# Batches 2 and 3 of a block-sparse attention: gathered keys and value rows, groups of 64 queries

## The chip, the core and the metric

The kernel runs on one core of one Trainium2 chip. A core has five engines that work side by side and wait for each other by semaphores: TensorE (PE, matmuls; its weight loads are shown as PEld), VectorE (DVE), ScalarE (ACT), GpSimd (POOL) and SyncE (SP, which here only issues DMAs). The metric is the device time of one execution in microseconds, as a median over runs.

## What is computed

Attention with a block mask (4 batches, 8 heads, 768 positions, 64 numbers per head), and then a layer of two matrix products on its output. Blocks are 32 positions long, so there are 24. A query block sees its own block and the two beside it, the first and the last block, and three blocks that a table names for it; the first and the last query block see everything.

```
scores = scale * q @ k.T
mask = abs(blk_i - blk_j) <= 1
mask = mask | (blk_i == 0) | (blk_j == 0) | (blk_i == 23) | (blk_j == 23)
for qb in range(24):
    for kb in sampled_blocks[qb]:              # 24 x 3 table
        mask[block qb, block kb] = True
attn = softmax(where(mask, scores, -1e9))
x = (attn @ v), heads side by side             # 3072 x 512
h = x @ w_in                                   # 512 x 2048
out = (max(h, 0) ** 2) @ w_out                 # 2048 x 512
```

## The kernel before

The numbers q, k and v are loaded by pairs of heads (a "unit" u; 16 units, four to a batch), cast to bf16 (`cast_qk`, `cast_v`) and transposed, so that QK holds queries and keys with the 2 x 64 numbers of the pair on the 128 partitions. Units 0 to 3 are transposed by TensorE, the others by DMA (`transp_dma`). In the loads, 6 successive positions lie on one partition, so a chunk of 128 keys holds every sixth position, from all blocks. No chunk can therefore be left out for a query, and the mask is laid over the full scores.

For each unit and each third of the queries (256) `scores` multiplies them with all six chunks of 128 keys; the two heads of a pair use the upper and the lower 64 rows of the PE array, by the helper `pair` (all its matmuls stand at L173). `exps` (L318) takes the exponential of two chunks at a time, 1024 numbers per partition, into pT. `masks` (L325) multiplies pT by the 0/1 mask MK, which is made once from the table by small matmuls; in the first third of batch 0, the mask is added to the scores instead. `values` multiplies pT by the value rows VT, which have a 65th column of ones, so that the sum of the weights comes along; some of units 0 to 3 use `values_full` (L358), which takes all 128 rows at once, the others the two row halves after each other. `normalize` divides (L365, L367), and the result is transposed into xT, by TensorE in batch 0 and by DMA afterwards.

The second part takes 256 tokens at a time (twelve tiles T). `hidden` multiplies by w_in, `relu` (L430, L432) and `square` (L441, L443) follow on ACT, DVE or POOL, `output` multiplies by w_out, `out_copy` and `store` bring the result out. This work on one batch is interleaved with the attention of the next.

The order of all of this is not left to a scheduler. Each step is a numbered task with its dependencies and buffers; the string PROGRAM lists all of them as words such as `P89/0` or `V24`: engine, task, and place in PSUM. Each engine executes its own words strictly in the order listed, and buffer counts (PT_BUFS, R_BUFS and so on) hold a task back until an older one has left its buffer.

Of the kernel before, what the change touches and what calls it, by code (L numbers as in the profile page):

```python
# [19 lines left out]
P = 128  # L20
# [5 lines left out]
def kernel(  # L26
# [32 lines left out]
    NRAW, NPB, QC_BUFS, XQ_BUFS, YS_BUFS = 4, 6, 5, 4, 3  # L59
    PT_BUFS, R_BUFS, G_BUFS, XT_BUFS, NX = 8, 3, 13, 3, 4  # L60
# [5 lines left out]
    scratch = dram.tile([1, 4], BF, name="scratch")  # L66
    ctx.enter_context(tc.manual_schedule())
# [49 lines left out]

    qv = q.rearrange("b (a t) (p n) d -> b a p t (n d)", t=2, p=P)
# [5 lines left out]
    def load(u, engs, e=None):  # L124
        b, a = divmod(u, HP)
        raw[u] = []
        for name, view, eng in zip(("qs", "ks", "vs"), (qv, kv, vv), engs):
            t = ld.tile([P, 2, NCH, D], F32, name=name, tag=name)
            eng.dma_start(out=t.rearrange("p t n d -> p t (n d)"), in_=view[b, a])
            raw[u].append(t)  # L130
# [5 lines left out]
    def load_part(eng, u, w, ns):  # L136
        if u not in raw:
            raw[u] = [ld.tile([P, 2, NCH, D], F32, name=n, tag=n) for n in ("qs", "ks", "vs")]
        eng.dma_start(out=raw[u][w][:, :, ns].rearrange("p t n d -> p t (n d)"),  # L139
                      in_=(qv, kv, vv)[w][0, u][:, :, ns.start * D:ns.stop * D])  # L140
# [22 lines left out]
    place = consts.tile([P, S], BF, name="place")  # L163
# [28 lines left out]
    QK, VT = [], []  # L192
    for i in range(NPB):
        QK.append(consts.tile([P, 2, S], BF, name=f"QK{i}"))
        VT.append(consts.tile([P, 2, NCH, 72], BF, name=f"VT{i}"))
        G.memset(VT[i][:, :, :, D:VW], 1.0)
# [34 lines left out]
    MK = consts.tile([P, NCH, S], BF, name="MK")  # L231
# [6 lines left out]
    def mask_evac(n, c0, c1, e):  # L238
        pk = mtile.pop((n, c0))
        if e == "ACT":  # L240
            A.activation(out=MK[:, n:n + 2, c0:c1], in_=pk, func=AF.Exp)
        else:
            V.tensor_scalar(out=MK[:, n:n + 2, c0:c1], in0=pk, scalar1=-1.0, scalar2=None, op0=AOP.is_ge)

# [11 lines left out]
    def cast_v(u, e):  # L256
        copy(e, VT[u % NPB][:, :, :, 0:D], raw[u][2])
# [63 lines left out]
    def masks(a, e):  # L321
        u, q0, w, cs = a
        pT = ptile[a].rearrange("p h (c q) -> p h c q", q=w)
        m = MK[:, cs[0]:cs[-1] + 1, q0:q0 + w]
# [5 lines left out]
    def values(slots, crossed, buf, e):  # L330
        u, q0, w, _ = slots[0]
        i = u % NPB
# [5 lines left out]
        for a in slots:  # L338
            pT = ptile.pop(a) if crossed else ptile[a]
            for j, n in enumerate(a[3]):  # L340
                for qc in range(w // P):
                    last = pair(lambda h: po[:, h, qc], lambda h, rows: pT[rows, h, j * w + qc * P:j * w + (qc + 1) * P],
                                lambda h, rows: VT[i][rows, h, n, 0:VW], crossed, start=not crossed and n == 0 and qc == 0,
# [4 lines left out]
    def values_full(slots, buf, e):  # L348
        u, q0, w, _ = slots[0]
        i = u % NPB  # L350
        otile[u, q0] = tile_of(buf)
        po = outs_of(otile[u, q0], w)
        for a in slots:
            pT = ptile.pop(a)
            for j, n in enumerate(a[3]):
                for h in range(2):
                    for qc in range(w // P):
                        nc.tensor.matmul(po[:, h, qc], pT[:, h, j * w + qc * P:j * w + (qc + 1) * P], VT[i][:, h, n, 0:VW],  # L358
# [20 lines left out]

    def x_evac(u, q0, w, e):  # L380
        b, a = divmod(u, HP)
        if b not in xT:
            xT[b] = work.tile([P, HP, S], BF, name="xT", tag="xT", bufs=XT_BUFS)
        copy(e, xT[b][:, a, q0:q0 + w].rearrange("r (c h p) -> r h c p", h=2, p=D), spare_of(otile.pop((u, q0)), w))

    def x_transp_dma(u, q0, w, e):
        b, a = divmod(u, HP)
        if b not in xT:
            xT[b] = work.tile([P, HP, S], BF, name="xT", tag="xT", bufs=XT_BUFS)
        sy.dma_start(out=xT[b][:, a, q0:q0 + w].rearrange("r (c p) -> r c p", p=P),  # L390
                     in_=xtile.pop((u, q0)).rearrange("p c h d -> p (c h d)"), transpose=True)
        otile.pop((u, q0))

# [13 lines left out]
    def hidden(T, f, part, parts, buf, e):  # L407
# [9 lines left out]
        for j, kc in work_[part % (parts // 2) * k_:(part % (parts // 2) + 1) * k_]:  # L417
            hlast[T, f] = pair(lambda i: htile[T, f][:, i, j * w:(j + 1) * w],
                               lambda i, rows: w_in_sb[rows, kc, (f + i * n + j) * P:(f + i * n + j + 1) * P],
                               lambda i, rows: xT[b][rows, kc, c0:c0 + w], crossed,  # L420
# [66 lines left out]
    def store(T, i, y, e):  # L487
        ts, n, cs = y
        sy.dma_start(out=ov[T[0], :, T[1] // P + ts:T[1] // P + ts + n, cs[0]:cs[1]],
                     in_=ystile.pop((T, i)).rearrange("p (n d) -> p n d", n=n))  # L490

# [6 lines left out]
    order = [(b * HP + a, q0, QW, cs) for b in range(B) for q0 in range(0, S, QW) for a in range(HP) for cs in CHUNKS]  # L498
    N0 = len(order) // B
    ev, cv, tr, sc_of, va_of, mu, mk, wl, gate, xb = {}, {}, {}, {}, {}, {}, {}, {}, {}, {}  # L500

    def prepare(u):
# [4 lines left out]
        if u >= HP:  # L507
            g = gate[GATES[min(u - HP, len(GATES) - 1)]]
            ld_t = T_(load, u, (sy, sy, sy), deps=cv[u - NRAW] + tr[u - NRAW] + [g])
# [22 lines left out]

    def attend(a, add):
# [7 lines left out]
        if not add:  # L541
            ex = T_(masks, a, deps=[ex] + [mk[n, c] for n in cs for c in range(q0, q0 + w, P)])
# [17 lines left out]
        kw = {}  # L560
        if b not in xb:
            xb[b] = Buf("xT")
            kw = dict(get=[xb[b]])
# [4 lines left out]
        mu[u, q0] = T_(x_evac, u, q0, w, deps=[xt], put=[ob[u, q0], ot], **kw)  # L568

# [9 lines left out]
    for u in range(NU):  # L579
        sc_of[u], va_of[u] = [], []  # L580
    for us in [range(b * HP, (b + 1) * HP) for b in range(B)]:
# [3 lines left out]
        if us[0] < HP:  # L585
            for c0, c1 in MASKED:
                for n in range(0, NCH, 2):
                    mb = Buf("X")
                    t = T_(mask_tile, n, c0, c1, mb, get=[mb], deps=mr)
                    x = T_(mask_evac, n, c0, c1, deps=[t], put=[mb])  # L590
                    for c in range(c0, c1, P):
                        mk[n, c] = mk[n + 1, c] = x
        for a in mine:
# [3 lines left out]
    for T in TILES:  # L597
        b, c0, tw = T
        n_u = per_unit(T)
        need = [mu[b * HP + a, q0] for a in range(HP) for q0, qw in QT if q0 < c0 + tw and c0 < q0 + qw]  # L600
        for f in range(0, NF, n_u):
            hb, ht, rb, gb = Buf("X"), Buf("H"), Buf("r"), Buf("g")
            last_use = c0 + tw == S and f + n_u == NF
            parts = 4
            hd = []
            for part in range(parts):
# [4 lines left out]
                             put=[xb[b]] if last_use and end else []))  # L611
# [20 lines left out]
        A18 P19/0 V24 P8/1 V21 P0/2 P25/3 P17/1 V20 A1 P6/1 P22/1 V26 G34 A23 P89/0 P9/2 P4/3 P35/1 A90 P12/2 P91/3 V36 V31 P93/2 A92  # L632
        P16/1 V44 P32/0 P13/1 V33 A94 V41 P103/1 P45/3 P42/0 A104 P101/2 V46 V30 P99/3 V54 V43 P95/1 A100 V51 A102 P55/0 P109/3 V56
        V96 P52/0 A110 G61 V53 P113/2 P97 P2/0 V98 A114 G40 P123/3 V3 P119/1 G50 A124 P75/0 P105/2 V76 G62 A120 P111/3 V27 G63 V106
        A112 P28/0 P121/1 G60 V29 P107 P73/0 A122 V108 P5/3 V37 P71/3 P115/2 G57 V74 A72 V47 P81/1 P38/0 P125/3 A82 V39 V116 P135/0
        G67 P11/1 V126 P117 P79/1 A136 V118 G64 V80 P127 P129/2 P132/0 A130 V128 G68 P48/1 V137 P777/3 V49 P778 A133 G65 V131 P142/2
        P58/1 P779 A143 V59 P145/0 V134 P780 P784/1 A146 V144 P161/2 P785 V781 A162 P148/0 P786 P787 A149 V147 G782 P155/2 P138/3 V788
        A156 P791/0 V163 A783 P158/1 P15/2 P792 V150 A159 S69 P174/2 S237 P793 V139 A175 P171/1 V160 P140 P794 V141 A172 V157 P151/2
        V176 A795 P168/3 P164/1 V173 A169 G796 V152 P181/0 V165 A182 P153 P798/3 V154 G66 V170 P166 P799 A797 S70 P184/2 V167 G790
        S243 P201/0 P177/1 A185 G789 A202 P800 V178 S249 P77/2 P801 A78 P179 P212/0 V180 V802 A213 P187/2 P821/1 P822 A188 P827/0 V183  # L640
        G803 P823 V186 A804 P198/3 P828 A199 P209/2 P824 P829 A210 V189 P815/3 V238 P816 A825 P190/2 V211 S239 P830 V214 P191 A831
        P817 V240 P215/1 P818 V192 A216 S241 P805/0 V200 A832 P193 V217 P195/1 P806 V203 A196 P807 V194 A819 V197 P223/2 P808 A224
        G820 P218/1 P204/3 A826 P809 P87/2 P205 G242 V88 P810 V206 G248 P226/2 V246 P219 A227 P207 P811 G250 V208 S247 V220 P229/3
        V244 P833/2 A230 P221 P834 V225 S245 P812 V252 P835 V228 A813 S251 P836 V222 P839/3 V231 A837 S253 P83/1 P264/0 P840 V84 G838
# [74 lines left out]
```

## Time and profile before

| | |
|---|---|
| median of 3 runs | 266.07 us (265.7 to 266.57) |
| profiled execution | 264.27 us, span on the core 262.5 us, granted TensorE clock 0.999 |
| PE busy | 251.1 us (96%), 5452 matmuls |
| ACT busy | 203.5 us (78%), of it 141.3 in 144 exponentials |
| DVE busy | 179.5 us (68%), of it 91.6 in 132 mask multiplications |
| POOL busy | 61.3 us (23%), of it 37.5 in 24 squarings |
| DMA | 37.20 MB, mean 142 GB/s |

The profile is one execution, and its span lies a little under the time of that execution; the median over runs is another 1.8 us higher. Busy time of PE is the union of its instructions' spans, and those overlap, as the array is a pipeline. How many matmuls really start per microsecond is read from the starts in the timeline.

### The profile page before, as it was taken

The page shows a single profiled execution, that of the slowest core. Times are in us where ns is not written, and L with a number is a line of the kernel's source. Part 1 is how long each engine was busy: PE and PEld are TensorE (multiplying, and loading weights), DVE is VectorE, ACT ScalarE, POOL GpSimd, SP SyncE. Part 2 cuts the span into 40 slices and gives each one's busy share as a digit, 9 for nine tenths or more (in the row PEclk, how much of TensorE's full clock was granted, in tenths as well). Part 3 has the DMA queues.
Part 4 walks back from the last instruction along what each step waited for, and adds up shares of the span by engine and source line. Part 5 has one row for each costly group of instructions (what it writes and reads, how often), then busy time and mean ns, then how long its engine had stood idle before and what let it go on. Part 6 is the DMA issues. An engine that isn't in the chain of part 4 may idle for free.

```text
span 262.5 us, 11968 instructions
## 1 busy us (share of the span) xinstructions
PE 251.1 (96%) x5452; PEld 204.0 (78%) x5452; DVE 179.5 (68%) x335; ACT 203.5 (78%) x222; POOL 61.3 (23%) x67
## 2 busy tenths in 40 slices
PE   8879969999999999999999999999999999999995
PEld 5667759777898798766789976698787697898884
DVE  6879988685899748866789965487676647851100
ACT  4988978959889979978889785678859879844660
POOL 3084252242025044400002140007104022014100
PEclk9999999999999999999999999999999999999999
DMA  6999999728989467918906947533001010640003
GB/s 189 367 260 201 207 296 315 143 51 199 267 232 301 117 84 133 292 32 137 240 15 153 218 167 102 131 76 111 13 13 24 3 22 20 215 145 13 0 37 129
DMA packets 50458, 37.20 MB, mean 142 GB/s; under 512 B 30824, under 2 KB 48872, under 8 KB 50408
## 3 DMA queue, kind: packets, MB, share of 16 engines
q1 hardware_dynamic: 45640, 31.86, 48.1%
q0 software_dynamic: 4224, 4.19, 9.9%
q8 instruction: 42, 0.69, 1.2%
q10 hardware_dynamic: 544, 0.39, 0.5%
q14 instruction: 8, 0.07, 0.1%
HBM read 27.26 MB, written 6.29 MB: 128 GB/s over the span
## 4 chain that ended last, share of the span: by engine, by line
PE 81%; DMA 7%; DVE 6%; SPq 2%; ACT 2%; POOL 1%; issue 1%; DVEq 0%; ACTq 0%
PE X L173 80%; DVE pT L325 3%; DMA vs<-in_v_dram 3%; DMA xT<-xq 2%; SPq L139 2%; DMA QK<-qc 2%; ACT pT L318 2%; PE X L358 1%; DVE r L432 1%; DVE xq L367 1%; DVE qc L115 0%; DVE xT L115 0%; POOL w_in_sb L286 0%; POOL VT L115 0%; PE X L264 0%
## 5 line engine op out<-in xcount | busy, mean ns | idle before, releaser
L318 ACT ACTIVATE pT<-X 128x1024 bf16<-128x1024 f32 x144 | 141.3, 1027 | 28.2 <-PE X L173 23.6
L173 PE MATMUL X<-xT,w_in_sb 64*128 64x256 bf16 x1536 | 100.8, 269 | 0.7 <-DMA xT<-xq 0.6
L325 DVE TENSOR_TENSOR pT<-pT,MK 128x1024 bf16<-128x1024 bf16 x132 | 91.6, 728 | 9.9 <-ACT pT L318 9.5
L173 PE MATMUL X<-w_out_sb,g 64*128 64x512 bf16 (+3 forms) x960 | 96.3, 333 | 0.1
L173 PEld LDWEIGHTS <-w_in_sb 64*128 64x128 bf16 x1536 | 78.6, 94 | 6.7 <-issue 1.0
L443 POOL TENSOR_TENSOR g<-r 128x1024 bf16<-128x1024 f32 (+1 forms) x24 | 37.5, 1569 | 165.7 <-ACT r L430 100.2
L173 PEld LDWEIGHTS <-g 64*128 64x128 bf16 x960 | 46.1, 94 | 21.4 <-ACT g L441 0.2
L173 PE MATMUL X<-QK 64*128 64x256 bf16 x576 | 56.0, 270 | 1.8 <-DVE QK L115 0.7
L173 PEld LDWEIGHTS <-pT 64*128 64x128 bf16 x1920 | 40.7, 94 | 4.5 <-issue 0.3
L432 DVE TENSOR_SCALAR r<-X 128x1024 f32<-128x1024 f32 x24 | 29.2, 1222 | 20.5 <-PE X L173 20.5
L173 PE MATMUL X<-VT,pT 64*128 64x65 bf16 x1920 | 42.7, 190 | 0.2 <-issue 0.2
L173 PEld LDWEIGHTS <-QK 64*128 64x128 bf16 x576 | 30.3, 94 | 12.2 <-issue 3.0
L441 ACT ACTIVATE g<-r 128x1024 bf16<-128x1024 f32 (+1 forms) x36 | 31.4, 891 | 6.3 <-DVE r L432 5.9
L430 ACT ACTIVATE r<-X 128x1024 f32<-128x1024 f32 x24 | 24.5, 1025 | 9.8 <-PE X L173 7.8
L365 DVE RECIPROCAL rs<-X 128x4 f32<-128x4 f32 x48 | 8.6, 179 | 24.9 <-PE X L173 22.1
L367 DVE TENSOR_TENSOR xq<-X,rs 128x256 bf16<-128x256 f32 x48 | 20.4, 425 | 1.7
L115 DVE COPY ys<-X 128x1024 f32<-128x1024 f32 (+1 forms) x5 | 5.2, 1038 | 15.1 <-PE X L173 15.0
L113 ACT COPY ys<-X 128x1024 f32<-128x1024 f32 (+3 forms) x10 | 8.3, 833 | 5.7 <-PE X L173 5.7
L358 PE MATMUL X<-VT,pT 128*128 128x65 bf16 x192 | 7.2, 193 | 3.3 <-DVE xT L115 2.2
L358 PEld LDWEIGHTS <-pT 128*128 128x128 bf16 x192 | 6.5, 97 | 4.7 <-DVE pT L325 2.3
L115 DVE CAST qc<-qs 128x768 bf16<-128x768 f32 (+2 forms) x16 | 9.0, 566 | 0.4 <-DMA qs<-in_q_dram 0.4
L115 POOL CAST VT<-vs 128x768 bf16<-128x768 f32 x8 | 7.2, 917 | 5.0 <-issue 5.0
(50 smaller groups left out, 83.7 us busy)
## 6 DMA issues: line engine op xcount, KB each, us to landing
vs<-in_v_dram SPq DMA_DIRECT2D x16, 384.0 KB, 6.7
ks<-in_k_dram SPq DMA_DIRECT2D x15, 384.0 KB, 5.8
out_dram<-ys SPq DMA_DIRECT2D x11, 512.0 KB, 4.7
qs<-in_q_dram SPq DMA_DIRECT2D x12, 384.0 KB, 5.0
w_in_sb<-in_moe_w_in_dram POOLq DMA_DIRECT2D x4, 512.0 KB, 7.1
w_out_sb<-in_moe_w_out_dram POOLq DMA_DIRECT2D x4, 512.0 KB, 11.5
qs<-in_q_dram SPq DMA_DIRECT2D x4, 256.0 KB, 7.4
xT<-xq SPq DMA_TRANSPOSE x36, 3.1
```

The costliest lines, as they stand in the source:

```text
L113: A.copy(out=out, in_=in_)
L115: (V if e == "DVE" else G).tensor_copy(out=out, in_=in_)
L173: last = nc.tensor.matmul(out(r ^ crossed), lhsT(r ^ crossed, rows), rhs(r ^ crossed, rows), skip_group_check=True, **kw)
L318: A.activation(out=pT[:, :, 0:n], in_=stile.pop(a)[:, :, 0:n], func=AF.Exp, scale=scale)
L325: V.tensor_tensor(out=pT, in0=pT, in1=m[:, None].broadcast_to([P, 2, len(cs), w]), op=AOP.mult)
L358: nc.tensor.matmul(po[:, h, qc], pT[:, h, j * w + qc * P:j * w + (qc + 1) * P], VT[i][:, h, n, 0:VW], start=n == 0 and qc == 0, stop=n == ...
L365: V.reciprocal(out=rs, in_=po[:, :, :, D:VW])
L367: V.tensor_tensor(out=xq.rearrange("p c h d -> p h c d"), in0=po[:, :, :, 0:D], in1=rs.broadcast_to([P, 2, n, D]), op=AOP.mult)
L430: A.activation(out=to, in_=src, func=AF.Relu)
L432: V.tensor_scalar(out=to, in0=src, scalar1=0.0, scalar2=None, op0=AOP.max)
L441: A.activation(out=g, in_=r, func=AF.Square)
L443: (G if e == "POOL" else V).tensor_mul(out=g, in0=r, in1=r)
```

## The change

In batches 0 and 1 the attention is as before. In batches 2 and 3:

- q, k and v are loaded in natural order: a chunk of 128 keys is four neighbouring blocks, and the loads consist of runs of 64 numbers (256 bytes) instead of 384 (1536 bytes).
- Queries are taken in 12 groups of 64. Group 0 holds the first and the last block and sees all six chunks. Groups 1 to 11 hold two neighbouring blocks and see three chunks: a window of 128 keys around them, and two chunks of 128 gathered keys (first block, last block, and the six blocks that the table names for the two). Two groups form a visit, six visits a batch.
- `k_gather`: POOL loads block numbers from the table into registers and copies the keys of those blocks, for all four units at once, to the tile kg: one copy for first and last block, six for the others, for each group.
- `v_store` writes the value rows of a batch (768 rows of 528 bf16 numbers, all heads) to DRAM; `v_gather` fetches 128 rows at a time by an indirect DMA from POOL, twice per group; `v_window` fetches 128 rows at a place known in advance, by SP.
- `s_scores`, `s_exps`, `s_masks` work on a visit of one unit: 2 groups x 3 chunks x 64 queries = 384 columns per head. The mask MKS is made once, by `table_slots` (24 small DVE operations), `table_spread`, `table_rows` and `table_masks`; it also clears what a block would count twice.
- `s_values` goes over all eight heads of a visit: stationary operand 128 keys x 64 queries, moving operand 65 columns, the two groups to partitions 0 to 63 and 64 to 127 of the result. `s_normalize` and `s_transp` take all heads at once, with tokens in a new order, which `store` undoes by the rows that it writes.
- Buffers: fewer of raw loads, qc, ys and g (3, 4, 2, 12 instead of 4, 5, 3, 13), one more xT, each now for a third of a batch; QK and the value rows now keep two batches. MK now lies in the buffers of the gathered value rows.
- PROGRAM is written anew, 1179 words instead of 1227. Of the squares 12 are on POOL (24 before) and 48 on ACT (36 before); ReLU is 30 times on ACT and 18 on DVE (24 each before).

The diff, cut to its core:

```diff
-    NRAW, NPB, QC_BUFS, XQ_BUFS, YS_BUFS = 4, 6, 5, 4, 3
-    PT_BUFS, R_BUFS, G_BUFS, XT_BUFS, NX = 8, 3, 13, 3, 4
+    NRAW, NPB, QC_BUFS, XQ_BUFS, YS_BUFS = 3, 2 * HP, 4, 4, 2
+    PT_BUFS, R_BUFS, G_BUFS, XT_BUFS, NX = 8, 3, 12, 4, 4
+    SB, VR, KG_BUFS, VG_BUFS = 2, D + 2, 2, 3
...
+    qn, kn, vn = [x.rearrange("b (a t) s d -> b a (t s) d", t=2).rearrange("b a (c p) d -> b a p c d", p=P) for x in (q, k, v)]
...
-        for name, view, eng in zip(("qs", "ks", "vs"), (qv, kv, vv), engs):
+        for name, view, eng in zip(("qs", "ks", "vs"), (qv, kv, vv) if b < SB else (qn, kn, vn), engs):
...
+    VISITS = [(2 * s, 2 * s + 1) for s in range(S // P)]
+    SL, RS = 12, 2 * n_rand
...
+    def table_rows(e):
+        V.tensor_scalar(out=idx, in0=low[1][:, P:3 * P].rearrange("p (c z) -> p c z", c=2)[:, :, 0:GR], scalar1=float(block), scalar2=lane,
+                        op0=AOP.mult, op1=AOP.add)
+
+    def table_masks(g0, g1, e):
+        copy(e, MKS[:, g0:g1].rearrange("p g c (a i) -> p (g c a) i", a=2), low[1][:, g0 * 6:g1 * 6, None].broadcast_to([P, (g1 - g0) * 6, block]))
...
+    def v_store(b, e):
+        sy.dma_start(out=rows_of[b].rearrange("(n p) c -> p n c", p=P), in_=VB[b % 2].rearrange("p n h c -> p n (h c)"))
...
+    def v_window(b, v, e):
+        g = VISITS[v][0]
+        sy.dma_start(out=vgt[b, v][:, 4], in_=rows_of[b][D * (g - 1):D * (g - 1) + P])
+
+    def v_gather(b, v, i, e):
+        g = VISITS[v][i]
+        for c in range(2):
+            G.indirect_dma_start(out=vgt[b, v][:, 2 * i + c], out_offset=None, in_=rows_of[b][:, :],
+                                 in_offset=bass.IndirectOffsetOnAxis(ap=idx[:, c, g - 1:g], axis=0))
+
+    def k_gather(b, v, e):
+        gs = [g for g in VISITS[v] if g]
+        j0 = (2 * gs[0] - 1) * n_rand
+        _, at = nc.values_load_multi_w_load_instructions(
+            tab[0:1, j0:j0 + RS * len(gs)], [mybir.EngineType.Pool], min_val=0, max_val=nb - 1,
...
+        kg = work.tile([P, HP * 4 * P], BF, name="kg", tag="kg", bufs=KG_BUFS).rearrange("p (a i c) -> p a i c", a=HP, i=2)
...
+        for g in gs:
+            to = kg[:, :, g % 2].bitcast(I32)
+            G.tensor_copy(out=to[:, :, 0:2 * w].rearrange("p a (j i) -> p a j i", i=w), in_=src.rearrange("p a (j i) -> p a j i", i=w)[:, :, 0:nb:nb - 1])
+            for r_ in range(RS):
+                G.tensor_copy(out=to[:, :, (2 + r_) * w:(3 + r_) * w], in_=src[:, :, bass.ds(at[(g - gs[0]) * RS + r_] * w, w)])
+
+    def s_scores(u, v, gs, buf, e):
+        b, a = divmod(u, HP)
+        i, ps, at = u % NPB, tile_of(buf), 0
+        for g in gs:
+            for c in range(chunks_of(g)):
...
+                pair(lambda h: ps[:, h, at:at + D], lambda h, rows: keys(rows), lambda h, rows: queries(rows), start=at == 0, stop=True)
+                at += D
+        stile[u, v, gs] = ps
+
+    def s_exps(u, v, gs, e):
+        n = sum(D * chunks_of(g) for g in gs)
+        pT = work.tile([P, 2, 512], BF, name="pT", tag="pT", bufs=PT_BUFS)
+        A.activation(out=pT[:, :, 0:n], in_=stile.pop((u, v, gs))[:, :, 0:n], func=AF.Exp, scale=scale)
...
+    def s_values(b, v, buf, e):
+        po = tile_of(buf)
...
+            for h in range(2):
+                cols = slice((2 * a + h) * VR, (2 * a + h) * VR + VW)
+                for c in range(NCH):
+                    for i, g in enumerate(VISITS[v]):
+                        if c >= chunks_of(g):
+                            continue
...
+                        nc.tensor.matmul(po[i * D:(i + 1) * D, h, a * VW:(a + 1) * VW], pts[g][:, h, c * D:(c + 1) * D], val,
+                                         start=a == 0 and c == 0, stop=c == chunks_of(g) - 1, skip_group_check=True)
...
+    def s_transp(b, v, e):
+        sy.dma_start(out=x_tile(b, v // 2 * QW)[:, :, v % 2 * P:v % 2 * P + P], in_=xtile.pop(("s", b, v)).rearrange("p a h d -> p (a h d)"), transpose=True)
...
+        cl = T_(v_claim, b, v, get=[vb], deps=mk_claims[-1:])
+        parts = [T_(v_gather, b, v, i, deps=[vw, cl, tb["rows"]]) for i, g in enumerate(VISITS[v]) if g]
+        if v:
+            parts.append(T_(v_window, b, v, deps=[vw, cl]))
+        kc = T_(k_gather, b, v, deps=[ev[u][1, 0] for u in us] + [tb["slots"]], get=[kb])
```

## The prediction

> **What bounds the kernel now.** I read the page first, for the busiest engine and its clock.
>
> ```profile
> span 262.5 us, 11968 instructions
> ...
> PE 251.1 (96%) x5452; PEld 204.0 (78%) x5452; DVE 179.5 (68%) x335; ACT 203.5 (78%) x222; POOL 61.3 (23%) x67
> ...
> PEclk9999999999999999999999999999999999999999
> ```
>
> TensorE is busy 96% of the span at its full granted clock. A busy PE need not be at its peak, so I took the pitch (start to start) of each form from PE's timeline: a row's start to the next row's start, over its count.
>
> ```profile
> 20.37 0.90 PE L358 MATMUL X<-VT,pT 128*128 128x65 bf16 x24
> 21.21 0.39 PE L173 MATMUL X<-QK 64*128 64x256 bf16 x4
> ...
> 22.98 0.29 PE L264 MATMUL X<-identb,qc 64*128 64x64 bf16 x8
> 23.10 1.05 PE L173 MATMUL X<-xT,w_in_sb 64*128 64x256 bf16 x16
> ...
> 203.88 0.38 PE L173 MATMUL X<-QK 64*128 64x256 bf16 x4
> 204.10 0.53 PE L173 MATMUL X<-VT,pT 64*128 64x65 bf16 x24
> 204.47 0.38 PE L173 MATMUL X<-QK 64*128 64x256 bf16 x4
> ```
>
> A 64x256 matmul costs 54.2 ns (0.22 us for 4; 0.867 for 16), a 64x65 one 15.4 ns (0.37 for 24), a 64x64 one 15: two row halves run at once, so each is half of about 31. A 128x65 on all rows has no partner: 30.9 ns. The groups by form give the counts, and the rows that price the new work.
>
> ```profile
> L318 ACT ACTIVATE pT<-X 128x1024 bf16<-128x1024 f32 x144 | 141.3, 1027 | 28.2 <-PE X L173 23.6 <-DVE xq L367 1.5 <-DVE pT L325 0.8
> L173 PE MATMUL X<-QK 64*128 64x256 bf16 x576 | 56.0, 270 | 1.8 <-DVE QK L115 0.7 <-issue 0.4 <-DMA QK<-qc 0.2
> L173 PE MATMUL X<-VT,pT 64*128 64x65 bf16 x1920 | 42.7, 190 | 0.2 <-issue 0.2
> L286 POOL DMA_DIRECT2D w_in_sb<-in_moe_w_in_dram x4 | 3.2, 793 | 0.0
> L283 POOL COPY held<-vs 1x2 f32<-1x2 f32 x1 | 0.2, 175 | 8.0 <-DMA vs<-in_v_dram 8.0
> ```
>
> Counts times pitches: hidden layer 1536 x 54.2 = 83.3; output 83.2 (704 at 108, the narrow ones in proportion); scores 576 x 54.2 = 31.2; values 1920 x 15.4 + 192 x 30.9 = 35.5; masks, transposes, warm-up 8.5. PE therefore has 241.7 us of work; 20.8 of the 262.5 are lost. Laying these pitches along the timeline, 13.8 are lost in the first 40 us, 3.4 from there to 240, the rest at the end. From 40 us on only PE work counts. The windows say what the first 40 wait for: ACT and DVE are the full engines, and DMA at times.
>
> ```profile
> 0.00:10.00 10.00, 7.70 (x129) 5.76 (x131) 6.92 (x24) 6.09 (x8) 2.08 (x17) 1.00 0.80 246
> 10.00:20.00 10.00, 8.40 (x179) 6.57 (x176) 7.94 (x18) 8.47 (x10) 5.96 (x9) 1.00 1.12 295
> 20.00:30.00 10.00, 9.52 (x204) 8.37 (x205) 9.84 (x21) 8.90 (x11) 4.36 (x5) 1.00 1.24 202
> 30.00:40.00 10.00, 7.59 (x160) 5.97 (x158) 8.67 (x17) 7.94 (x10) 3.84 (x4) 1.00 1.16 270
> ```
>
> To place other work I walk the order that is written out in the kernel (its entries are called words below) and add up PE's pitches: a place in it is given as PE's work up to there.
>
> **PE's part of the change.** In batches 2 and 3 a head pair's 12 query groups take 6 + 11 x 3 = 39 key chunks instead of 6 chunks of all 768 queries.
> - Scores: 288 matmuls of 64x256 go (15.6 us); 8 pairs x 39 x 2 = 624 of 64x64 come, at 15.4 (9.6): -6.0.
> - Values: 1152 of 64x65 go (17.7); 16 heads x 39 = 624 come, 65 columns on 128 rows, with 64 output partitions that alternate between the halves of the array's columns. No row shows column halves at work. If two run at once as row halves do, 15.4 each: 9.6, gain 8.1. If not, the row is the 128x65 one, 30.9: 19.3, loss 1.6. I take the first: like the row halves, two matmuls on disjoint parts of the array write disjoint parts of PSUM.
> - The 12 value steps leave the 64-row tiling. At 20.37 the 24th matmul starts at 21.08 and the next form at 21.21: about 0.1 us over the pitch, and an estimate of as much on entry; 12 x 0.2 = +2.4 (bounds 0 and 5).
>
> PE's sum: -11.7, or -2.0 without overlap. [...] That is the first rival below.
>
> **ACT.** 72 exponentials of 1027 ns go; 48 of 768 elements (0.81, on the line through the 512-element row, 597, and the 1024-element one) and 8 of 384 (0.49) come: -31. But the order written out changes too: POOL's squares fall from 24 to 12 and ACT takes 12 more, and six more ReLUs. Batches 0 and 1, still whole, are squeezed together: ACT's words listed ahead of PE's 90th microsecond of work sum to 104 at row means, against 94. ACT's records overlap (141.3 busy for 148 summed), so 99 against 90. Before, PE reached that point at 105 us. ACT was idle 8.6 of the first 40 (windows), so now 99 + 8.6 = 108: 3 later. With both engines nearly full I take +5 (2 to 8).
>
> **DVE and tables.** 24 small table operations between 0.06 and 0.30 (the 24-partition rows), 3.2 taken, and 1.5 for a mask copy and the row numbers. Over PE's first 20 us of work DVE's words sum to 26.0 against 27.0, since other steps moved: nothing added; were they uncovered, +5. Later 72 mask multiplies become 48 shorter ones and 24 normalizations 12: DVE is nowhere late.
>
> **POOL.** This is the new load: 22 group steps of 7 copies of 64 or 128 elements and 6 register loads, and 44 indirect loads; all have to pass in order through POOL, with 3.7 us of casts, between PE's words at 90.8 and 196.3 us of work. Anything late holds the squares, casts and gathers behind it, then the score and value words. Copies: six memsets start 43 ns apart, a lone copy takes 175, so 0.1 to 0.3; 0.2 taken. Register loads: no row; a register MOVE took 39 ns, a DMA instruction 793; 0.15 taken, as it is nearer to the MOVE. Indirect loads: the DMA row says 0.79 at 512 packets, the slowest 0.93; here 128 rows but indices to read: 0.4 to 1.6, taken 0.93. Sum: 22 x (1.4 + 0.9) + 41 + 4 = 96. Room: 105.5 + 2.4 of drains + some 5 by which gathers lie ahead of their users = 113. Hidden.
>
> **SP and DMA.** 24 loads now come in 256-byte pieces: 1536 packets at 27 ns instead of 256 at 78 (trace means) over 16 DMA engines, 2.6 us instead of 1.25, with the loads 10 us or more ahead: hidden (otherwise +1.4 each). The value table goes out and comes back: store about 4.7 (the 512 KB output row), two gather issues 1.9, landing about 3: 10 us, where the order leaves 13.4 of PE's work between the store and the first value step: hidden, by 3. SP's transposes are equal in bytes, 12 wide for 24.
>
> **Sum.** Span 262.5 - 11.7 + 5 = 255.8. The profiled execution took 264.27 (1.8 around its span), and the median is 266.07, another 1.8; so 266.07 - 6.7 = 259.4. Own range 255 to 264: the 2 to 8 of ACT, drains 0 to 5.
>
> **Rivals.**
> 1. *Column halves take turns.* PE gains 2.0 only, less 5 for ACT: 269. For it: the only 128-row row is 30.9. Against: the row halves' 15.4. [...]
> 2. *POOL becomes the bound* (the other side). It decides once POOL's work passes 113: a register load above 0.28 (0.13 x 132 = 17), or an indirect load above 1.3. At 0.4 per register load POOL needs 129: 16 late, 275; at 0.8, 182, so over 320. For it: half of its price has no row. Against: 23% busy now, and its waits are for work of others:
>
> ```profile
> POOL g L443 <- ACT r L430: 100.2, 12, 24.5
> ```
>
> 3. *ACT eats it all*: through batches 0 and 1 ACT, not PE, sets the pace and 12 are lost there instead of 5: 266, no change. Against: ACT's 99 against PE's 90 leave room only for 3.
>
> That fewer matmuls would not result can't be: the loops are fixed at 3 chunks.
>
> **Numbers.** Forecast 0.55, rival 1 0.13, rival 2 0.24, rival 3 0.08. A measurement tells 0.3% (0.8 us) apart. Faster: 0.51 of the forecast, 0.04 of rival 2 (POOL late by a few microseconds only), 0.01 of rival 1: 0.56. Same: 0.07, mostly rival 3. Slower: 0.37. The range reaches from below the forecast's own, 254 (ACT nothing late), into rival 2 (POOL 22 late), 281.
>
> **What would show it.** Right: value matmuls of 65 columns at 15 ns pitch, PE work near 230 us, POOL idle between gathers. Wrong: value pitch near 30 (rival 1); PE idle behind kg copies, with POOL over 95% busy or issuing between 95 and 205 us (rival 2); PE idle behind ACT before 100 us (rival 3).

## The result and the profile after

The changed kernel takes 270.9 us (median of 20 runs, 265.95 to 273.6), the kernel before 266.15 in the same comparison. The ratio, 1.014 with an interval of 1.010 to 1.019, counts only executions within 1.5% of each kernel's fastest (8 and 13 of the 20, means 269.0 and 265.2 us), here and in all that follows. (On some other chips the changed kernel is far slower, 1.204 in e9 below.) I had forecast 259.4. Its profiled execution took 270.82, with a span of 268.7; the busiest engine and its clock on the page:

```profile
span 268.7 us, 11960 instructions
...
PE 248.2 (92%) x5268; PEld 185.7 (69%) x5268; DVE 153.6 (57%) x308; ACT 189.6 (71%) x224; POOL 117.2 (44%) x257
...
PEclk9798599999999999959999999999999999999998
```

TensorE is no longer full, and its clock, which was granted whole before (0.999 on average), is granted at half in three stretches (7.5 to 10.9, 24.5 to 34.8 and 113.3 to 120.1 us) and at the very end. The work that it has did shrink as forecast. PE's timeline of one value step and of the scores of two head pairs (columns: start, time, engine, line, operation, count):

```profile
145.05 0.22 PE L573 MATMUL X<-vg,pT 128*64 128x65 bf16 x1
145.05 0.22 PE L573 MATMUL X<-VB,pT 128*64 128x65 bf16 x1
145.10 0.26 PE L573 MATMUL X<-vg,pT 128*64 128x65 bf16 x5
...
145.93 0.61 PE L185 MATMUL X<-xT,w_in_sb 64*128 64x256 bf16 x8
```

```profile
139.92 0.19 PE L185 MATMUL X<-QKT 64*128 64x64 bf16 x2
139.95 0.22 PE L185 MATMUL X<-QKT,kg 64*128 64x64 bf16 x4
...
140.27 1.47 PE L185 MATMUL X<-xT,w_in_sb 64*128 64x256 bf16 x24
```

The value step's first two matmuls, on the two column halves, start together; its 48 take 0.88 us, 16 ns each and 0.1 for entering and leaving. 24 score matmuls take 0.35, 15 ns each. Counts times pitches now give 228.2 us of work, against 241.4 before with the same accounting: about 13 saved (scores 288 x 54.2 less 624 x 15 ns, 6.2; values 1152 x 15.4 less 624 x 16, 7.8; less 0.1 for each of 12 value steps). So 40.5 of the span are lost where 21.1 were; PE's work is priced at full clock, so half clock counts as lost. Where they lie, with four runs that are told below:

| Kernel | PE's work | lost up to 40 us | 40 to 130 | 130 to 240 | later |
|---|---|---|---|---|---|
| before | 241.4 | 13.8 | 1.8 | 1.6 | 3.9 |
| changed | 228.2 | 19.7 | 11.2 | 5.0 | 4.6 |
| before, with 256-byte loads (e8) | 241.4 | 13.9 | 9.4 | 2.0 | 3.8 |
| changed, with long loads (e1) | 228.2 | 17.6 | 6.1 | 8.5 | 4.6 |
| plain gathers, no tables (e18) | 228.1 | 14.2 | 10.9 | 5.5 | 4.7 |
| the same, with long loads (e17) | 228.1 | 15.2 | 5.2 | 5.8 | 4.6 |

The windows of the changed kernel show the two places (columns: window, length, busy time of PE, PEld, DVE, ACT, POOL with counts, granted clock, DMA share, GB/s):

```profile
20.00:30.00 10.00, 5.71 (x102) 4.07 (x103) 7.44 (x33) 6.86 (x9) 5.59 (x8) 0.73 1.19 174
...
110.00:120.00 10.00, 6.15 (x102) 4.82 (x100) 4.57 (x9) 4.17 (x5) 0.00 (x0) 0.66 0.69 144
```

At 110 us PE's timeline names a transfer, and SP's issue queue says why it is late:

```profile
110.71 0.27 PE L185 MATMUL X<-xT,w_in_sb 64*128 64x256 bf16 x2
113.95 0.40 PE L185 MATMUL X<-xT,w_in_sb 64*128 64x256 bf16 x2 [2.97 <-DMA xT<-xq]
115.23 1.46 PE L185 MATMUL X<-xT,w_in_sb 64*128 64x256 bf16 x12 [0.88 <-DMA xT<-xq]
```

```profile
104.11 1.34 SPq L136 DMA_DIRECT2D qs<-in_q_dram  x1
105.55 0.65 SPq L136 DMA_DIRECT2D ks<-in_k_dram  x1
106.25 2.31 SPq L136 DMA_DIRECT2D vs<-in_v_dram  x1
108.65 5.37 SPq L406 DMA_TRANSPOSE xT<-xq  x3
```

The loads of one head pair in 256-byte pieces hold SP's queue for 4.3 us, and the three transposes that PE waits for stand behind them. In the kernel before, such loads go by faster:

```profile
122.42 0.57 SPq L129 DMA_DIRECT2D qs<-in_q_dram  x1
123.04 0.46 SPq L129 DMA_DIRECT2D ks<-in_k_dram  x1
123.54 0.48 SPq L129 DMA_DIRECT2D vs<-in_v_dram  x1
```

All 24 loads in pieces take 38 us of issue time, on average 1.2 (qs), 1.4 (ks) and 2.2 us (vs), single ones from 0.42 to 3.75; in the kernel before they take 0.5 to 0.66 on average. SP issues for 150 us instead of 124 in all, and in stretches of ten microseconds from 60 to 160 us it is 77 to 97% full (92 on average, 66 before). The DMA engines are full at that place too:

```profile
104.00:108.00 4.00, 4.00 (x113) 3.67 (x110) 3.03 (x7) 3.98 (x5) 1.05 (x1) 1.00 1.08 141
108.00:112.00 4.00, 2.98 (x72) 2.52 (x67) 3.91 (x6) 4.00 (x5) 0.84 (x1) 1.00 1.18 217
```

At 20 us PE waits for a cast on POOL, then for DVE, which is busy with the table steps from 23.2 to 28.4:

```profile
22.55 0.29 PE L281 MATMUL X<-identb,qc 64*128 64x64 bf16 x8 [1.78 <-POOL qc L118]
...
29.59 0.29 PE L393 MATMUL X<-identb,xq 64*128 64x64 bf16 x4 [1.80 <-DVE xq L382]
```

```profile
23.22 0.18 DVE L447 COPY tab<-sb_r 1x72 int32<-1x72 int32 x1
...
28.16 0.27 DVE L466 CAST r<-ids 11x256 bf16<-11x256 f32 x1
...
28.56 0.42 DVE L382 TENSOR_TENSOR xq<-X,rs 128x256 bf16<-128x256 f32 x1
...
29.11 0.42 DVE L382 TENSOR_TENSOR xq<-X,rs 128x256 bf16<-128x256 f32 x1
```

The half clock from 24.5 to 34.8 us begins 2 us after the first of these waits and has the second inside it; the one from 113.3 to 120.1 begins within the wait at 111. The wait at 20.8 us and 10 of these 17 us at half clock are not typical: of the 20 executions this one has the lowest mean clock (0.958; the others 0.968 to 0.993), and e2 and e4, which leave the table steps and the loads as they are, have no wait at 20.8 and 6.8 us at half clock between 12 and 260 us.

### The profile page after: what moved, and what is told of

Same layout as the page of the kernel before. It is cut to its first block, busy times and chain, and to the rows that moved or that the text cites. A ratio compares the mean times of both kernels' runs of the same rounds, so it can differ in the third digit from the quotient of the medians.

```text
span 268.7 us, 11960 instructions
## 1 busy us (share of the span) xinstructions
PE 248.2 (92%) x5268; PEld 185.7 (69%) x5268; DVE 153.6 (57%) x308; ACT 189.6 (71%) x224; POOL 117.2 (44%) x257
## 4 chain that ended last, share of the span: by engine, by line
PE 71%; DMA 11%; DVE 7%; ACT 5%; issue 2%; SPq 2%; POOL 1%; POOLq 0%; DVEq 0%; ACTq 0%
PE X L185 66%; DMA kg<-in_q_dram 6%; PE X L573 4%; DMA xT<-xs 2%; DVE pT L342 2%; ACT r L623 2%; ACT pT L335 2%; DMA vg<-rows,idx 2%; SPq L151 1%; DMA xT<-xq 1%; DVE xq L382 1%; SPq L406 1%; PE X L373 1%; DVE MKS L118 0%; ACT g L634 0%
## 5 line engine op out<-in xcount | busy, mean ns | idle before, releaser
L335 ACT ACTIVATE pT<-X 128x1024 bf16<-128x1024 f32 x72 | 70.4, 1026 | 10.2 <-PE X L185 9.6
L543 ACT ACTIVATE pT<-X 128x768 bf16<-128x768 f32 (+1 forms) x56 | 41.5, 763 | 27.5 <-PE X L185 25.2
L500 POOL DMA_INDIRECT vg<-rows,idx x44 | 44.4, 1008 | 12.2 <-issue 11.3
L185 PE MATMUL X<-QKT 64*128 64x256 bf16 (+1 forms) x560 | 45.1, 239 | 2.5 <-DVE QKT L118 1.2
L342 DVE TENSOR_TENSOR pT<-pT,vg 128x1024 bf16<-128x1024 bf16 x60 | 40.5, 713 | 4.6 <-ACT pT L335 4.6
L550 DVE TENSOR_TENSOR pT<-pT,MKS 128x768 bf16<-128x768 bf16 (+1 forms) x48 | 26.1, 583 | 21.6 <-ACT pT L543 21.6
L185 PEld LDWEIGHTS <-QKT 64*128 64x128 bf16 x560 | 25.5, 96 | 9.7 <-issue 2.5
L517 POOL COPY kg<-QKT 128x64 int32 x132 | 28.0, 257 | 0.0
L185 PEld LDWEIGHTS <-pT 64*128 64x128 bf16 x768 | 15.8, 95 | 3.3 <-DVE pT L342 0.5
L515 POOL COPY kg<-QKT 128x128 int32<-128x128 int32 x22 | 7.1, 323 | 24.8 <-DMA QKT<-qc 14.2
L185 PE MATMUL X<-VB,pT 64*128 64x65 bf16 x768 | 17.3, 191 | 0.3 <-DVE pT L342 0.2
L573 PEld LDWEIGHTS <-pT 128*64 128x64 bf16 x624 | 11.7, 111 | 4.2 <-issue 3.3
```

The source lines that it names most:

```text
L185: last = nc.tensor.matmul(out(r ^ crossed), lhsT(r ^ crossed, rows), rhs(r ^ crossed, rows), skip_group_check=True, **kw)
L335: A.activation(out=pT[:, :, 0:n], in_=stile.pop(a)[:, :, 0:n], func=AF.Exp, scale=scale)
L342: V.tensor_tensor(out=pT, in0=pT, in1=m[:, None].broadcast_to([P, 2, len(cs), w]), op=AOP.mult)
L500: G.indirect_dma_start(out=vgt[b, v][:, 2 * i + c], out_offset=None, in_=rows_of[b][:, :], in_offset=bass.IndirectOffsetOnAxis(ap=idx[:, c ...
L517: G.tensor_copy(out=to[:, :, (2 + r_) * w:(3 + r_) * w], in_=src[:, :, bass.ds(at[(g - gs[0]) * RS + r_] * w, w)])
L543: A.activation(out=pT[:, :, 0:n], in_=stile.pop((u, v, gs))[:, :, 0:n], func=AF.Exp, scale=scale)
```

## Experiments

The theory after the first profile (A): two steps that I had called hidden cost the gain, the 256-byte loads in SP's queue and the table steps at the start, each with half clock behind it. Rivals: POOL's gathering; the bytes in the DMA engines; the alternation of the column halves. Ratios are against the kernel before on the same chip, with 95% intervals.

**e1: long loads in the changed kernel.**

```diff
-        ... zip(("qs", "ks", "vs"), (qv, kv, vv) if b < SB else (qn, kn, vn), engs):
+        ... zip(("qs", "ks", "vs"), (qv, kv, vv), engs):
```

> Batches 2 and 3 are loaded in runs of 1536 bytes as batches 0 and 1 are; the gathered keys and values are then other positions, so this computes something else at the same cost. Queue theory (SP, which issues loads and transposes one after the other, is full from 60 to 160 us because each load in 256-byte pieces occupies it for 1.2 to 2.2 us instead of 0.5): the 24 loads give back some 25 us of SP, the wait for the transposed x at 111 us goes, and the time falls by 6 to 10 us from 271. Start theory (what is lost is lost in the first 40 us) and POOL theory: less than 2 us.

265.1 us, 0.995 (0.991 to 0.999), where the changed kernel has 1.014: by the ratios about 5 us less, a little under the queue theory's 6 to 10 and well over the 2 of the others. SP issues for 119 us, and the wait at 110 us is gone. (Of the 8.5 us that the table has from 130 on, 3.1 are one stall at 133 us without a named wait. POOL issues no indirect load in it, so it is not of the kind told at e9.)

**e2: the held copy before the first weight load** (`if i == 0` becomes `if i == 1` in the weight load).

> The small copy that holds the first weight load back until the values of unit 2 are in now stands before the load that POOL really issues first. Start theory: the last part of unit 3's queries lands 1 to 3 us earlier than 21.8, the wait at 20.5 shrinks, the clock is granted in full there, and the time falls by 2 to 3 us. Queue theory: within 1 us.

270.7, 1.021 (1.013 to 1.029): no gain. The wait at 20.8 us is gone and 17.2 us are lost up to 40, but the unedited start of e1 and e4 loses 17.6 without that wait too (19.7 in the first profile), so the copy's place is worth little; there are still waits at 110 and 150 us.

**e3: the table words in the middle of the second batch** (words 23 to 27 moved, one scratch tile less).

> The small DVE table steps and the mask copies move from batch 0 to the middle of batch 1, where they are early enough for the first gather; they share one r buffer instead of holding two. Start theory: the 5.1 us of DVE at 23.3 to 28.4 leave the chain, PE does not wait 2.2 us at 27.4, the clock stays full, and the time falls by 3 to 6 us. Queue theory: 0 to 2 us, as the first transposes come earlier but the SP queue sets the pace afterwards.

271.7, 1.027 (1.020 to 1.034): no gain either. The start loses 15.0 instead of 17.6 to 19.7, without half clock from 12 us on, but the waits go along with the words:

```profile
87.59 0.54 PE L185 MATMUL X<-VB,pT 64*128 64x65 bf16 x24 [3.62 <-DVE r L625]
```

**e4: no alternation between the column halves.**

```diff
-                for c in range(NCH):
-                    for i, g in enumerate(VISITS[v]):
-                        if c >= chunks_of(g):
-                            continue
+                for i, g in enumerate(VISITS[v]):
+                    for c in range(chunks_of(g)):
```

> The value matmuls of a visit run through one group's chunks and then the other's, so that neighbours use the same half of the array's columns. If the halves run at once when they alternate, 312 pairs lose their partner: 624 x (31 - 16) ns = 9 us more TensorE work and 4 to 9 us more time. If they never ran at once: no difference.

271.1, 1.022 (1.015 to 1.029): no difference that the intervals show, and PE's timeline shows the two halves starting 10 ns apart still:

```profile
143.63 0.22 PE L571 MATMUL X<-vg,pT 128*64 128x65 bf16 x1
143.64 0.22 PE L571 MATMUL X<-VB,pT 128*64 128x65 bf16 x1
```

**e5 to e8** ran on a second chip. e5 joins e1, e2 and e3. e6 lets POOL issue the 24 loads (`(sy, sy, sy) if u < SB * HP else (nc.gpsimd,) * 3`). e7 is e6 with e2 and e3. e8 is the kernel before with its loads of the third and fourth batch in 256-byte pieces:

```diff
-        for name, view, eng in zip(("qs", "ks", "vs"), (qv, kv, vv), engs):
+        for name, view, eng in zip(("qs", "ks", "vs"), (qv, kv, vv) if b < 2 else (qn, kn, vn), engs):
```

> Three edits together: the third and fourth batch are loaded in runs of 1536 bytes (other positions of the sequence, so the values are not those of the reference), the held copy stands before the first weight load, and the table words stand in the middle of the second batch. Theory A (SP's queue and the start are two separate losses that add up): the loads give 5 us (their run alone 265.1 against 270.9), and the start some 3 to 5 more where nothing waits behind SP any longer: 260 to 262, ratio 0.98 to 0.985; half clock nowhere between 12 us and 260. Rival B (the start is given back whatever SP does): 265, as with the long runs alone, and new waits near 80 to 100 us where the tables now stand. Rival C (POOL): 265 with waits behind kg copies or gathers after 120 us.

> The changed kernel with the 24 loads of the third and fourth batch issued by POOL (GpSimd) instead of SP; pieces, positions and bytes stay. Theory A (what costs is that the transposes wait behind these loads in SP's queue, not the pieces in the DMA engines): SP's issue time falls from 150 to about 112 us, no wait of 3 us for xT at 110 us, total 265 to 268. Rival B (the small pieces cost in the DMA engines): transposes are late still, 270 to 272. Rival C (POOL has no room for 24 issues of about 1 us each beside its gathers): SP is free, but score and value words wait behind kg and vg after 120 us, 272 or more.

> The run with the loads by POOL, and besides the held copy before the first weight load and the table words in the middle of the second batch. All of the reference is computed. Theory A (losses add up): 3 to 5 us below the run with the loads by POOL alone, 261 to 264. Rival B (the start's gain is given back by waits of its own at the new place of the tables, 84 to 97 us): the same as the run with the loads by POOL alone, within 1 us.

> The kernel before with one edit: the 24 loads of the third and fourth batch take the sequence in pieces of 256 bytes (other positions, so the values are not those of the reference). This prices my forecast's step that the short pieces are hidden. Theory A (what counts is that SP is full): SP's issue time rises by 26 us from 124 to about 150, but SP was 44 to 80% full, so it costs only part of the 5 us that the long runs gave back in the changed kernel: +1 to +4. Rival B (hidden when nothing else is added): within 0.8 us of before.

e8: 272.7, 1.026 (1.017 to 1.034), so the pieces alone cost 6.8 us, more than either theory gave them. SP issues for 151 us (124 before). From 60 to 160 us its queue goes from 66 to 86% full, the DMA engines from 75 to 80%. The wait is of the same kind:

```profile
97.62 0.28 PE L177 MATMUL X<-xT,w_in_sb 64*128 64x256 bf16 x2 [3.86 <-DMA xT<-xq]
```

e5, e6 and e7 came out at 316.7, 330.1 and 337.8 (1.189, 1.238 and 1.261), which neither theory had. On e6 one thing can be read from before POOL's gathers begin: a load costs POOL 1.0 to 1.1 us, PE waits 1.6 and 5.0 us for `QKT<-qc` up to 66.6 and 74.0 us, and by 130 us it has lost 38.6 where the changed kernel has lost 30.9. Another issuing engine did not help in this run. It also speaks against theory A as it stood. SP issues for only 110 us in e6 and none of the 24 loads stands in its queue, yet the issue of one transpose takes 5.5 us at 69.8 (minimum, median and maximum in ns, from 56 to 82 us):

```profile
L288 SPq DMA_TRANSPOSE QKT<-qc x6: 1211/1342/5470, 57.9 to 75.4; - x6
```

The DMA engines are full there (shares of 1.02 to 1.30 in stretches of four microseconds from 56 to 80 us). So how much of the price is the place in SP's queue, and how much is engines that the loads fill, these runs do not separate. e6 speaks against the queue alone. For the queue speak e8 and the engines' shares in the kernel before and e17: they are as full there between 104 and 116 us (up to 1.33 and 1.25), and PE waits for a transpose there 0.7 us at most. The rest of e5 to e7 is stalls without a named wait, so the changed kernel itself was run as a control.

**e9 to e12**, on a third chip: e9 the changed kernel as it is; e10 e5 again; e11 with POOL's gathering made plain:

```diff
-            G.indirect_dma_start(out=vgt[b, v][:, 2 * i + c], out_offset=None, in_=rows_of[b][:, :],
-                                 in_offset=bass.IndirectOffsetOnAxis(ap=idx[:, c, g - 1:g], axis=0))
+            G.dma_start(out=vgt[b, v][:, 2 * i + c], in_=rows_of[b][P * c:P * c + P])
...
-        _, at = nc.values_load_multi_w_load_instructions(
...
+        at = [1 + r_ for r_ in range(RS)] * len(gs)
```

e12 with the load words of three head pairs (445, 439, 578) behind the transposes that followed them.

> The changed kernel as it is, as a control. The three runs that should have gained (long runs with an early held copy and late tables; loads by POOL, twice) came out at 316, 330 and 338 us, all on one chip, with stalls of 0.7 us in TensorE's instruction issue that fall together with POOL's indirect loads. Theory A (these stalls come with indirect loads on some chips, or in some placements, whatever else is edited): if this control shows them, it is 300 or more; if not, it is 269 to 272, and the next run (the same kernel as the first of those three) is 260 to 265. Rival B (the edits themselves bring the stalls): control 269 to 272 and the next run 315 again.

> The same kernel as in the run of long loads with the held copy early and the tables late, once more, beside a control. Theory A (chip): 260 to 265 where the control is near 270. Rival B (the edits bring the stalls): 315 again, with 28 us of stalls inside the series of indirect loads.

> The changed kernel with POOL's gathering made plain: the 44 indirect loads become ordinary loads of 128 rows from fixed places, still issued by POOL, and the key copies read fixed places, without register loads (so the keys and values of the gathered blocks are not those of the reference). Rival 2 of the prediction (POOL's register loads and indirect loads cost time): several microseconds below the control. Theory A (POOL's new work lies beside PE's): within 1 us of the control; POOL busy 25 us less. Where the control shows stalls in TensorE's issue, this run tells whether indirect loads make them.

> The changed kernel with three of SP's words moved: the load words of the eleventh, twelfth and thirteenth head pair stand behind the transposes of xq that followed them (one, one and three words). All of the reference is computed. Theory A (the wait of 4.5 us and the half clock near 110 us come from transposes queued behind these loads): that wait is gone, 266 to 268. Rival B (it is the bytes in the DMA engines, or the wait moves to the next transposes): 269 to 272, with a wait for xT or QKT elsewhere between 90 and 160 us.

e9: 318.7, 1.204 (1.189 to 1.220); e10 319.3; e12 319.5; e11 273.3, 1.025 (1.007 to 1.044). On this chip the unedited changed kernel is 20% slower than the kernel before, which takes 265.6 on it as everywhere. So e5's edits are not what brings the stalls, and e10 and e12 say nothing on what their own edits are worth. e9's PE and POOL at the same time:

```profile
152.59 0.19 PE L573 MATMUL X<-vg,pT 128*64 128x65 bf16 x1
153.25 0.27 PE L573 MATMUL X<-vg,pT 128*64 128x65 bf16 x4 [0.47 <-issue]
...
154.02 0.24 PE L573 MATMUL X<-vg,pT 128*64 128x65 bf16 x3 [0.47 <-issue]
```

```profile
152.50 0.95 POOL L500 DMA_INDIRECT vg<-rows,idx  x1 [0.30 <-issue]
153.75 0.94 POOL L500 DMA_INDIRECT vg<-rows,idx  x1 [0.30 <-issue]
```

While POOL issues indirect loads, PE gets one to five matmuls every 0.7 us, waiting for nothing that the profile names. Gaps of over 0.55 us from one matmul's start to the next that begin in those series sum to 36 us in e9, 34 in e10, and 1.3 in the changed kernel's first profile; besides, e9's clock is at half for over 40 us (17 in that profile). e11, without indirect and register loads, has no such series on the same chip. It is also 273, no faster than the changed kernel where that is undisturbed, so no cost of the gathering shows there (its interval is 4% wide).

e9's own trace points to one of the two kinds of load. Laid against POOL's records, PE is idle for 13.0 of the 29.7 us in which an indirect load runs alone, for 3.3 of the 12.9 us in which one runs beside a register load, and for 0.8 of the 19.7 us in which a register load runs alone. e10 and e12 have the same shares within a few hundredths.

**e13 to e16**, on a fourth chip: e13 only the indirect loads made plain; e14 only the register loads gone, with fixed places for the keys; e15 e11 with e5's edits; e16 e11 with e12's moves.

> The changed kernel with its 44 indirect loads made ordinary loads of 128 rows from fixed places by POOL; the register loads and the key copies at register places stay (the gathered values are not those of the reference). Theory A (the indirect loads bring the stalls): 271 to 274, no series of 0.7 us stalls, on any chip. Rival B (the register loads bring them): on a chip that shows the stalls, 300 or more.

> The changed kernel with key copies from fixed places and no register loads; the 44 indirect loads stay (the gathered keys are not those of the reference). Theory A (the indirect loads bring the stalls): on a chip that shows them 310 to 320 with 25 us or more of stalls inside the series of indirect loads; on a chip without them 269 to 272. Rival B: 271 to 274 on any chip.

> POOL's gathering made plain (no indirect loads, no register loads), and besides the third and fourth batch loaded in runs of 1536 bytes, the held copy before the first weight load, and the table words in the middle of the second batch (the values are not those of the reference). Theory A (the losses by the 256-byte loads and at the start add up): 260 to 264, against 273 with plain gathering alone. Rival B (the start's gain is given back where the tables now stand): 265 to 268, from the loads alone.

> POOL's gathering made plain, and the load words of the eleventh, twelfth and thirteenth head pair behind the transposes of xq that followed them (the values are not those of the reference). Theory A (the wait near 110 us is a matter of the order in SP's queue): 268 to 270 against 273 with plain gathering alone. Rival B (SP is full in that stretch, so the wait moves to the next transposes): 272 to 274, with a wait of 2 us or more for QKT or xT between 95 and 125 us.

e13: 271.8, 1.017 (1.009 to 1.025). e14: 269.2, 1.007 (1.002 to 1.012), with its indirect loads in place and 3.1 us of gaps in their stretches; there was no control on this chip, so a chip without stalls can't be told from stalls that only register loads make. e15: 270.6, 1.012 (1.006 to 1.017): the start loses 15.2, but PE waits 3.6 us at 84.7 and 0.8 and 1.5 at 96.8 and 99.2, where the tables now stand. That is rival B's mechanism, at a price 3 us above its 265 to 268. e16: 272.2, 1.019 (1.010 to 1.028), rival B too: the wait has moved to the next transposes behind the same three loads.

```profile
107.00 0.58 SPq L136 DMA_DIRECT2D qs<-in_q_dram  x1
107.68 0.65 SPq L136 DMA_DIRECT2D ks<-in_k_dram  x1
108.38 3.14 SPq L136 DMA_DIRECT2D vs<-in_v_dram  x1
111.56 5.48 SPq L288 DMA_TRANSPOSE QKT<-qc  x3
```

```profile
121.41 0.35 PE L185 MATMUL X<-QKT 64*128 64x64 bf16 x12 [3.38 <-DMA QKT<-qc]
```

**e17 and e18**, on a fifth chip, take the losses out instead of moving them: gathering plain, the held copy early and the table steps left out (`return` at the head of each, the masks set to one by POOL instead); e17 with long loads besides.

> POOL's gathering plain, the third and fourth batch loaded in runs of 1536 bytes, the held copy before the first weight load, and the six table steps left out (their masks are set to one by POOL at 120 us or so; values are not those of the reference). What is left of the change is TensorE's part and POOL's copies and loads. Theory A (these two losses are what kept the forecast's 12 us from showing): 257 to 261, ratio 0.965 to 0.98; no half clock between 12 us and 260. Rival B (the gain is lost in many places, by ACT or by waits that move on): 264 to 268.

> As the run before it, but with the third and fourth batch loaded in pieces of 256 bytes as in the changed kernel. Theory A: 5 to 8 us above that run (the price of the pieces, 6.9 in the kernel before and 5.8 in the changed one), so 263 to 268, and 4 to 6 below the run with plain gathering alone (272 to 273), which is the price of the table steps at the start. Rival B (what is saved at the start is given back in SP's full stretch from 60 to 125 us, since PE only arrives there earlier): 270 to 273.

e17: 261.6, 0.983 (0.978 to 0.988), just above theory A's 257 to 261; e18: 268.1, 1.004 (0.999 to 1.009). e17's page:

```profile
span 258.9 us, 11761 instructions
...
PE 243.0 (94%) x5260; PEld 181.8 (70%) x5260; DVE 146.1 (56%) x282; ACT 188.4 (73%) x223; POOL 101.7 (39%) x250
...
PEclk9999999999999999999999999999999999999999
```

The clock is whole again. By the ratios, the loads are worth 5.5 us on one chip (e18 less e17, 2.1%; 6.8 in e8, 5 in e1). The table steps are worth 3.5 to 5.7 (e13 and e11 less e18; the held copy, edited with them, had changed nothing alone). That second price is rough: it is taken across chips, and the two differences carry intervals of 2.5 and 5 us to each side. At their later place the tables cost 7.6 (e15 less e17, also across chips). With both losses out, the median is 2 us above the forecast.

## Why the prediction was wrong

- **TensorE, -11.7: right.** About 13 by the same accounting, with values at 16 ns (taken 15.4) and about 0.1 us a step for entering and leaving (the forecast's "drains", taken 0.2; the runs show this time, not what it consists of). Rival 1 is out: the column halves ran at once, their matmuls starting in pairs 3 ns apart from 145.05 on, and the 30.9 ns of matmuls on all rows was the wrong row to price them by.
- **SP and DMA, "hidden": the step that failed first.** I priced the pieces by bytes and packets in the DMA engines, 1.4 us a load, and looked whether the loads themselves would land in time. They did: after 60 us only one cast waits for a load (15.4 us, on POOL), and no row of PE names a wait for one. What I left out is that the issuing instruction holds SP's queue for 1.2 to 2.2 us on average instead of 0.5 to 0.66, and that the transposes of xq, xs and qc, which PE does wait for, stand behind it: 26 us more on SP, 5 to 7 us of the end. That the pieces cost this is shown by e1, by e8 and by e17 beside e18. That it is the queue is argued from where the waits lie; e6 leaves open how much of it the full DMA engines make. e16, with another order of the same words, handed the wait to the next transposes (3.4 us at 121.4) while SP was full.
- **DVE and tables, "nothing added": failed.** The bracket had the size, "uncovered, +5" (3.5 to 5.7). That DVE's words summed to no more than before over PE's first 20 us says nothing of one chain of 5.2 us standing ahead of the word that PE waits for.
- **The clock: no term at all.** I took the pitches at the full clock (0.999) that the page of before showed. From 12 us to 258 the changed kernel's profile has 17 us at half clock at and behind the waits, e2 and e4 have 7, and e17, without these waits, has none. Granted at 0.5, it can lose at most half of its length, so 8.5 us in that profile and 3.4 in the others; it is part of the two prices above, not a third one.
- **ACT, +5: over in size, and not shown in kind.** From 40 to 100 us e17 loses 3.2 where the kernel before lost 1.1, so about 2, the lower end of 2 to 8, for all causes together; PE's waits for ACT that the profile names there are two of 0.2 us. The changed kernel's 4.3 there hold SP's part too. Rival 3, which needed 12, is out.
- **POOL, "hidden": right, with prices off both ways.** The groups and the waits of the changed kernel:

```profile
L500 POOL DMA_INDIRECT vg<-rows,idx x44 | 44.4, 1008 | 12.2 <-issue 11.3 <-PE X L185 0.8
...
L517 POOL COPY kg<-QKT 128x64 int32 x132 | 28.0, 257 | 0.0
```

```profile
POOL vg L500 <- issue: 11.3, 40, 0.3
...
POOL kg L515 <- issue: 9.7, 2, 5.0
```

An indirect load is 1.0 us and 0.3 behind it (taken 0.93; rival 2 decided at 1.3), a series of 12 register loads 1.4 to 5.4 us with a median of 2.9, so 0.24 each (taken 0.15; it decided at 0.28), but these run beside earlier work of POOL. Both prices came close to what I had named as deciding, so that POOL stayed hidden owes something to luck. Without register loads e14 is some 2 us faster than the changed kernel or e13, on intervals that overlap; without either kind (e11) nothing is won that its interval shows. What indirect loads or register loads do to PE's issue on two of the chips (36 us of gaps in e9) is another matter; no step of mine had it.
- **From 130 us on, nothing lost: missed by about 4.** e17 still loses 5.8 from there to 240, where 1.6 were lost before: 1.4 us for `QKT<-qc` at 178.5 and many gaps below 1 us. Which of them belong to what part of the change was not taken apart.

## What to carry over

A DMA's price had three parts here: its bytes (1.4 us more for a load in pieces, an estimate from the packet times before), its landing (3.1 us for a transpose of xq before), and the time that its issue held the queue, 0.5 to 0.66 us on average for a load in long runs and 1.2 to 2.2 in 256-byte pieces. Where a change cuts transfers into short pieces, list what stands behind them in that queue and how full it is in that stretch, not on average. And where the bounding engine is at 96%, each small wait that a change brings can be paid again if the clock falls behind it, as with the two waits of 1.8 us here and the 10.3 us of half clock: look for steps that nothing in the trace covers at their very place, not in a sum over 20 us.

## Hardware that I had not expected

- **The clock fell after short waits, but not after every one.** Between 12 and 40 us, one idle time of PE of 1.9 to 2.2 us is followed or overlapped by 3.4 us of half clock in e1, e2, e4, e13 and e14, and in the changed kernel's first profile two of 1.8 us by 10.3; in the kernel before one of 2.2 us up to 38.2, and in e3 one of 3.6 us up to 87.6, by none. Away from the ends, every stretch of half clock in these traces is 3.4 us long or two or three times that. The length of the wait alone does not decide in these traces, as shorter ones came with half clock and a longer one did not. What decides stays open here.
- **Matmuls on the two column halves started out of the program's order** in e4: at 143.63 and 143.64 us, with two matmuls of the first group written between them. Writing them alternately gained nothing that the intervals show (1.014 with it, 1.022 without).
- **PE's issue stalled while POOL issued indirect loads:** 0.7 us per one to five matmuls, 36 us of gaps in e9 and 48 us more than in the first comparison, on the chips of e5 to e7 and e9 to e12, and 1 to 4 us of gaps on the others. The kernel before, without such loads, ran alike on all (265.6 to 266.8 us). With plain loads and fixed places (e11, 273.3 us on such a chip) there is no such series. e9's trace has the gaps under indirect loads and hardly any under register loads alone; no run took away just one of the two on a chip that stalls, and what differs between the chips stays open. The verdict of 1.4% is therefore that of undisturbed chips.
